# Moving most of a fused kernel's activation loads from SyncE's to GpSimd's DMA queue, and its GELU table load to a later place

## The chip, the core and the metric

One core of one Trainium2 chip. The time is that of one execution on the device in microseconds (us). A time quoted for a kernel is the median of its runs. A trace is taken of one execution by the hardware profiler; its span is some 1.7 us shorter than the run's time. A run over 1.5% above the fastest of its kernel counts as slow.

In the views PE is TensorE (PEld its weight loads), DVE VectorE, ACT ScalarE, POOL GpSimd and SP SyncE. Of TensorE's products, ps_t are transposes, ps_s scores, ps_o outputs of the attention, ps_kv the state from k and v, ps_h and ps_out the two layers of the MLP, and ps_fill products of zeros that keep it busy.

## The reference, cut to what matters

The kernel fuses decaying linear attention with a two-layer MLP. The attention takes q, k, v of shape 4 batches x 8 heads x 768 positions x 64, in float32, block by block of 64 positions; its output is the input of the MLP.

```python
for b in range(nb):                                  # 12 blocks of 64 positions
    intra = einsum(qb, kb) * Dmask                   # within the block
    intra = einsum(intra, vb)
    inter = einsum(qb * lam_pow, kv_state)           # from the blocks before
    out[:, :, sl] = intra + inter
    kv_state = lam_block * kv_state + einsum(kb * rev_pow, vb)
...
h = x @ w_in                                         # 3072 x 512 by 512 x 2048
g = h * sigmoid(1.702 * h)
return g @ w_out                                     # 2048 x 512
```

## The kernel before

The work goes in six "waves" of positions. In waves 0 and 1 (`w < ND`, ND is 2) each half `c` of a wave is the first 256 positions of one batch, from wave 2 on 128 positions of two batches. "Batch 0" and "batch 1" in the texts are the two halves `c` of a wave. The landing buffers kf, qf, vf are float32 tiles of 4096 bytes on each of 128 partitions. The weights go through GpSimd's queue and are converted to bf16 on the way. The k, q and v go through SyncE's, except for one.

```python
def load_one(w, c, nm, src):
    x = ld.tile([P, H, 2 * D], f32, tag=f"{nm}{c}", name=f"{nm}f")
    if w < ND:
        n = H if w or (nm == "v" and c) else H // 2
        for h in range(0, H, n):
            (nc.gpsimd if w == 0 and c and nm == "v" else nc.sync).dma_start(out=x[:, h : h + n], in_=...)
    else:
        nc.sync.dma_start(out=x.rearrange(...), in_=...)
...
    behind = const.tile([1, 2], bf16)        # where the gates write
    behind_q = const.tile([1, 1], f32)
...
def gate_pool(x):                            # GpSimd goes on when x has landed
    nc.gpsimd.tensor_copy(behind_q, x)
def gate_sync(x):                            # SyncE's queue goes on when x has landed
    nc.sync.dma_start(out=behind, in_=x)
...
# for wave 1, batch 0, GpSimd casts v (in two halves); for batch 1 it casts k, and ScalarE v
((pool_copy, pool_copy), (act_copy, act_copy))[c]
...
if w + 2 < NW:                               # wave w+2 is loaded n+20 items into wave w (w = 0)
    side += [(n + (12 if w else 20), (load, w + 2))]
```

## Time and profile before

| | before |
|---|---|
| median of 3 runs | 207.61 us (207.47 to 208.85) |
| span of the profiled run | 206.6 us (its time was 208.35, so it is one of the slower runs) |
| TensorE busy | 96% of the span |
| TensorE's waits at wave 1's start (ps_kv) | none |

The main lines are in the prediction below. Two more rows of the page belong to them: each digit is one fortieth of the span, in tenths of full speed (PEclk, the granted clock of TensorE) or of the busy time of the 16 DMA engines.

### The profile page before, as it was taken

How to read it: one execution, taken by the hardware profiler on the slowest of the kernel's cores; microseconds unless marked ns; L12 is line 12 of the kernel's file. 1: busy time of each engine (PE TensorE's matmuls, PEld its weight loads, DVE VectorE, ACT ScalarE, POOL GpSimd, SP SyncE). 2: the span in 40 equal slices, each digit the busy share in tenths (PEclk: the TensorE clock that was granted, in tenths of full speed). 3: DMA queues.
4: the chain of work that ended last, by engine and by line, in shares of the span. 5: the costliest groups of instructions: out<-in, count | busy, mean ns of one | idle time of the engine just before them, and what ended most of it. 6: DMA issues, size and time to landing. Idle time of an engine off the chain costs nothing.

```text
span 206.6 us, 4263 instructions
## 1 busy us (share of the span) xinstructions
PE 199.1 (96%) x1802; PEld 105.3 (51%) x1825; DVE 89.3 (43%) x160; ACT 86.1 (42%) x158; POOL 17.1 (8%) x38
## 2 busy tenths in 40 slices
PE   7989999999999999999999999999999999999994
PEld 2657544467864464444464444464444454444453
DVE  1784000686952842932743931743841731100121
ACT  4857662157665030565030566021566021565000
POOL 4469000140000000000000000000000000000000
PEclk9999999999999999999999999999999999999999
DMA  5999999999997999979981379961360111100112
GB/s 156 314 232 197 195 206 257 316 274 228 210 226 182 213 261 235 217 169 224 257 234 51 110 180 264 232 184 52 102 151 3 46 59 51 51 0 0 54 51 102
DMA packets 86744, 33.82 MB, mean 164 GB/s; under 512 B 67398, under 2 KB 83654, under 8 KB 86726
## 3 DMA queue, kind: packets, MB, share of 16 engines
q1 hardware_dynamic: 81828, 28.84, 55.2%
q0 software_dynamic: 4896, 4.72, 13.6%
q8 instruction: 14, 0.23, 0.4%
q14 instruction: 4, 0.03, 0.1%
q10 hardware_dynamic: 2, 0.00, 0.0%
HBM read 27.26 MB, written 6.29 MB: 162 GB/s over the span
## 4 chain that ended last, share of the span: by engine, by line
PE 89%; DMA 3%; SPq 3%; DVE 3%; issue 1%; ACT 0%; ACTq 0%
PE ps_out L418 39%; PE ps_h L394 35%; PE ps_h L406 5%; DMA qf<-in_q_dram 3%; SPq L81 3%; PE ps_s L332 2%; PE ps_o L382 2%; PE ps_o L369 1%; DVE o_sb L422 1%; PE ps_t L235 1%; DVE sm L264 1%; PE ps_o L313 1%; PE ps_kv L356 1%; PE ps_s L256 1%; PE ps_o L295 1%
## 5 line engine op out<-in xcount | busy, mean ns | idle before, releaser
L418 PE MATMUL ps_out<-w_out,g_sb 128*128 128x512 bf16 (+2 forms) x400 | 83.8, 362 | 1.1 <-issue 0.6
L394 PE MATMUL ps_h<-xT,w_in 128*128 128x512 bf16 x330 | 73.2, 379 | 0.3
L396 ACT ACTIVATE g_sb<-ps_h 128x512 bf16<-128x512 f32 x84 | 50.1, 597 | 45.2 <-PE ps_h L394 45.2
L418 PEld LDWEIGHTS <-g_sb 128*128 128x128 bf16 x416 | 38.2, 98 | 41.0
L394 PEld LDWEIGHTS <-w_in 128*128 128x128 bf16 x336 | 32.9, 98 | 39.2
L422 DVE COPY o_sb<-ps_out 128x512 f32<-128x512 f32 (+2 forms) x26 | 16.9, 650 | 53.0 <-PE ps_out L418 50.2
L340 DVE SCALAR_TENSOR_TENSOR sm<-ps_s,inv_pow,mask 128x512 bf16<-128x512 f32 x32 | 21.8, 743 | 28.5 <-PE ps_s L332 22.3
L386 ACT CAST xT<-ps_o 128x512 bf16<-128x512 f32 x16 | 8.2, 600 | 37.8 <-PE ps_o L382 37.8
L199 DVE TENSOR_TENSOR ks<-kf,kd_pow 128x256 bf16<-128x256 f32 x8 | 2.9, 420 | 20.6 <-DMA kf<-in_k_dram 17.3
L406 PE MATMUL ps_h<-xT,w_in 128*128 128x256 bf16 x96 | 11.4, 273 | 0.0
L206 DVE TENSOR_TENSOR qs<-qf,q_pow 128x512 bf16<-128x512 f32 x16 | 10.3, 682 | 0.0
L206 DVE TENSOR_TENSOR ks<-kf,k_pow 128x512 bf16<-128x512 f32 x16 | 10.3, 682 | 0.0
L406 PEld LDWEIGHTS <-w_in 128*128 128x128 bf16 x96 | 9.0, 98 | 1.6 <-DVE xT L215 0.2
L264 DVE TENSOR_TENSOR sm<-ps_s,mask_d 128x512 bf16<-128x512 f32 x14 | 8.8, 683 | 0.9 <-PE ps_s L256 0.8
L408 ACT ACTIVATE g_sb<-ps_h 128x512 bf16<-128x512 f32 x12 | 7.2, 598 | 4.3 <-PE ps_h L406 4.3
L144 PE MATMUL ps_fill<-zero 128*128 128x512 bf16 x14 | 6.7, 576 | 1.5 <-DVE zero L114 1.4
L360 DVE SCALAR_TENSOR_TENSOR kv<-kv,blk_pow,ps_kv 128x256 bf16<-128x256 bf16 x12 | 5.0, 476 | 6.0 <-PE ps_kv L356 6.0
L218 ACT COPY kT<-ps_t 128x512 bf16<-128x512 bf16 (+1 forms) x4 | 3.2, 796 | 7.7 <-PE ps_t L235 7.6
L199 DVE TENSOR_TENSOR qs<-qf,qd_pow 128x256 bf16<-128x256 f32 x16 | 5.8, 419 | 1.3 <-DMA qf<-in_q_dram 1.3
L332 PEld LDWEIGHTS <-kT 64*128 64x128 bf16 x128 | 3.6, 94 | 3.4 <-issue 3.4
L215 DVE CAST v_sb<-vf 128x1024 bf16<-128x1024 f32 x8 | 5.1, 683 | 0.0
L332 PE MATMUL ps_s<-qT,kT 64*128 64x128 bf16 x128 | 5.0, 217 | 0.0
(69 smaller groups left out, 93.4 us busy)
## 6 DMA issues: line engine op xcount, KB each, us to landing
kf<-in_k_dram SPq DMA_DIRECT2D x10, 512.0 KB, 5.8
qf<-in_q_dram SPq DMA_DIRECT2D x10, 512.0 KB, 6.5
vf<-in_v_dram SPq DMA_DIRECT2D x10, 512.0 KB, 6.7
out_dram<-o_sb SPq DMA_DIRECT2D x15, 256.0 KB, 2.0
out_dram<-o_sb SPq DMA_DIRECT2D x17, 128.0 KB, 2.4
w_out<-in_moe_w_out_dram POOLq DMA_DIRECT2D x4, 512.0 KB, 12.7
kf<-in_k_dram SPq DMA_DIRECT2D x4, 256.0 KB, 3.1
qf<-in_q_dram SPq DMA_DIRECT2D x4, 256.0 KB, 5.1
```

Of the source, the lines that this page charges most:

```text
L199: eng.tensor_tensor(x.rearrange("p a (r i j d) -> p r j i a d", i=2, j=2, d=D)[:, R, j], f[:, h].rearrange("p i (a d) -> p i a d", a=2), p ...
L206: eng.tensor_tensor(x.rearrange("p b (r i j d) -> p j (b r) i d", i=2, j=2, d=D)[:, j], f.rearrange("p h (a d) -> p (h a) d", a=2).rearran ...
L264: nc.vector.tensor_tensor(sm.rearrange("p i a s -> p i (a s)"), flat, mask_d.rearrange("p o a b s -> p o (a b s)").to_broadcast([P, 2, 2 * ...
L332: nc.tensor.matmul(s2[h][:, b, :], kT[hs, (b % 2) * NP + p, :], qT[hs, (b % 2) * NP + p, :], start=True, stop=True)
L340: nc.vector.scalar_tensor_tensor(sm, s, inv_pow[:, n : n + 1], mask.to_broadcast([P, B, P]), op0=MUL, op1=MUL)
L386: nc.scalar.copy(xT[w][:, p, :], ps_o.rearrange("p b s -> p (b s)"))
L394: nc.tensor.matmul(h, w_in_sb[j][:, kc, i * P : (i + 1) * P], xT[w][:, kc, :], start=(kc == 0), stop=(kc == KC - 1))
L396: nc.scalar.activation(g_of[w][:, fc, :], h, GELU)
L406: nc.tensor.matmul(h[:, u, :], w_in_sb[j][:, kc, i * P : (i + 1) * P], xT[w][:, kc, cols], start=(kc == 0), stop=(kc == KC - 1))
L408: nc.scalar.activation(g_of[w][:, fc : fc + 2, cols], h, GELU)
L418: nc.tensor.matmul(ps_out, g_of[w][:, fc, g * P : (g + 1) * P], w_out_sb[j][:, fc % CW, c0:c1], start=(fc == 0), stop=(fc == FFC - 1))
L422: nc.vector.tensor_copy(o, ps_out)
```

## The change

The intent: give nearly all loads of the first 50 us to one issuer in one order, so that nothing has to be gated, start batch 1's loads of wave 0 earlier, and take the GELU table load out of ScalarE's busiest stretch.

```diff
-                (nc.gpsimd if w == 0 and c and nm == "v" else nc.sync).dma_start(
+                (nc.gpsimd if w or c else nc.sync).dma_start(
...
-            nc.sync.dma_start(out=x.rearrange(...),
+            (nc.gpsimd if w == ND else nc.sync).dma_start(out=x.rearrange(...),
...
-                    if w or c == 0 or nm != "v":
+                    if w or c == 0:
...
-    behind = const.tile([1, 2], bf16)
...
-    def gate_sync(x):
-        nc.sync.dma_start(out=behind, in_=x)
...
-        nc.scalar.activation(warm, q_pow[:, 0, 0:1], GELU)
+        gate_pool(loaded[0, 0, "k"][0:1, H // 2, 0:1])
+        load_one(0, 1, "k", k)
+        load_one(0, 1, "q", q)
+        load_w_in(0)
+        load_one(0, 1, "v", v)
...
-        for nm, copies in (("k", (dve_copy, act_copy)), ("q", (act_copy, dve_copy))):
+        for nm, copies in (("k", (act_copy, act_copy)), ("q", (act_copy, dve_copy))):
...
-                fill(2 - g if nm == "k" else 1 - g)
-        gate_pool(loaded[0, 0, "q"][0:1, H // 2, 0:1])
-        load_w_in(0)
-        load_one(0, 1, "v", v)
+                fill(1 if nm == "k" else 1 - g)
         cast_v(0, 0, (act_copy, act_copy))
+        nc.scalar.activation(warm, q_pow[:, 0, 0:1], GELU)
...
-        fill(3)
+        fill(2)
...
-        gate_sync(w_out_sb[1][0:1, 0, 0:2])
         load(1)
...
-                side += [(n + (12 if w else 20), (load, w + 2))]
+                side += [(n + (12 if w else 8), (load, w + 2))]
```

More of the change, by code (lines that the diff above doesn't have):

```diff
@@ L84, in load_one @@
         else:
-            nc.sync.dma_start(out=x.rearrange("p h (a d) -> p (h a) d", a=2),
+            (nc.gpsimd if w == ND else nc.sync).dma_start(out=x.rearrange("p h (a d) -> p (h a) d", a=2),
                               in_=src[2 * c : 2 * c + 2, :, w * P : (w + 1) * P, :].rearrange("b h s d -> s (b h) d"))
```

## The prediction

> **What bounds the kernel now.** I read the page's engine shares first, then the chain of work that ended last in order of time, and then the start of the kernel engine by engine. The chain's summary:
>
> ```profile
> span 206.6 us, 4263 instructions
> PE 199.1 (96%) x1802; PEld 105.3 (51%) x1825; DVE 89.3 (43%) x160; ACT 86.1 (42%) x158; POOL 17.1 (8%) x38
> PE 89%; DMA 3%; SPq 3%; DVE 3%; issue 1%; ACT 0%; ACTq 0%
> ```
>
> TensorE is 96% busy and 89% of the chain. A transfer is only 3% of it. In order of time (columns: start, duration, what):
>
> ```profile
> 6.21 0.65 SPq L81
> 6.85 0.04 issue
> 6.90 6.48 DMA qf<-in_q_dram
> 13.38 0.02 issue
> 13.40 0.77 DVE qs L199 x2
> 14.17 0.05 issue
> 14.22 0.40 PE ps_t L235 x4
> ...
> 15.24 2.08 DVE sm L264 x4
> 17.32 0.04 issue
> 17.36 0.31 PE ps_o L313 x8
> ...
> 18.57 2.78 PE ps_h L406 x24
> ...
> 203.59 0.29 DVE o_sb L422
> ```
>
> From 18.57 us to 203.59 us the chain is matmuls, one after another, apart from three waits of 0.70 us for an output copy, which the change does not touch. So a change of loads can win only in the first 18.57 us, and there only along q of batch 1: issued last on SyncE, landed at 13.38, cast, transposed, scored, masked, multiplied. Everywhere else it can at best do no harm. GpSimd's timeline shows what the change will load up (start, duration, instruction; in brackets idle time before it and its releaser):
>
> ```profile
> 7.00 0.23 POOL L453 COPY behind_q<-qf 1x1 f32<-1x1 f32 x1 [3.63 <-DMA qf<-in_q_dram]
> 7.17 0.95 POOL L178 DMA_DIRECT2D w_in<-in_moe_w_in_dram  x1
> 8.11 0.92 POOL L81 DMA_DIRECT2D vf<-in_v_dram  x1
> 9.85 2.32 POOL L199 TENSOR_TENSOR ks<-kf,kd_pow 128x256 bf16<-128x256 f32 x4 [0.81 <-ACT v_sb L218]
> 12.12 1.55 POOL L178 DMA_DIRECT2D w_in<-in_moe_w_in_dram  x2
> ...
> 40.39 1.16 POOL L212 CAST v_sb<-vf 128x512 bf16<-128x512 f32 x2 [19.62 <-DMA vf<-in_v_dram]
> ```
>
> One issue keeps GpSimd 0.75 to 0.95 us, also for the 1024 rows of v (0.92). At 40.39 it casts wave 1's v as soon as that lands. Its reader on TensorE (v_sb is an operand) follows closely:
>
> ```profile
> 42.89 0.44 PE L276 MATMUL ps_kv<-v_sb,ks 64*64 64x64 bf16 x16
> ```
>
> **What the Trainium skill says.** (1) "DMA: Bandwidth & Descriptors", Issuing engines are not separate DMA queues: all issuers share the same 16 engines; another issuer saves only sequencer time. Its section Queues, rings and completion order adds that each engine goes round-robin between queues, packet by packet. The first agrees with the trace, the second hardly: between 31 and 34 us, with wave 1's loads issued on SyncE from 30.85 us behind the weights on GpSimd's queue, the DMA view has
>
> ```profile
> q0 software_dynamic: 619, 0.62, 123.5%
> q1 hardware_dynamic: 5, 0.00, 0.3%
> ```
>
> (packets, MB written, share of the engines). So the order is close to the order of issue, whichever the queue. Likewise w_in, issued at 7.17, has no packet before 10 us, while q1 works off its backlog. (2) The same page, Latency and other measured facts, gives about 1 us to the first byte for GpSimd and 0.6 us for SyncE. Here w_in, issued at 12.12 into a nearly empty queue, shows packets from about 14.1: 2 us. (3) "ScalarE: Activation LUTs", What ACT_TABLE_LOAD costs: 1283 ns and a drain of 1380 ns. The trace has 1.28 us for the load and the next instruction right at its end, with no drain seen. (4) "SBUF — State Buffer", SBUF: two separate sides: a vector op in a two-port mode keeps GpSimd from writing descriptors. In the start VectorE runs two-input products and PSUM copies, and the issues there took under 0.95 us, so I add nothing.
>
> **The change part by part.**
>
> Queue of batch 1, wave 0. Removed: four SyncE issues (4.18 to 7.82) and the gate on q. Added: a gate on the second half of k (issued at 1.33, some 3.0 us to landing, so about 4.4) and six GpSimd issues in a row. Estimate: gate copy 0.2, then six issues of 0.75 to 0.95 from about 4.7: GpSimd free at 9.6 to 10.2, against 9.03 before. First packet of k at 4.7 + 2.0 = 6.7, or later; batch 0's 1.57 MB (1.03 MB by 6 us, 0.65 MB from 6 to 8) is through at about 7.7, so nothing starves. The order k, q, w_in, v is the order of issue before, too; the gain is that w_in and v no longer run among the tail of q. By 10 us 2.33 MB had moved; batch 0 plus batch 1's k and q are 2.62 MB; at 0.32 MB/us the rest is through at 10.9. Last data to semaphore was 1.3 us (q's packets nearly gone at 12.1, landed 13.38), so q lands at about 12.2, not 13.38: 1.1 us earlier. VectorE is at its masks until 12.13 before. GpSimd's own casts of k end at 12.2 to 12.6 as before (12.17).
>
> Table behind the v casts. Removed from ScalarE: 1.28 + 0.20 us at 5.80 to 7.29. Added: the same after the v casts. The gap there is 1.52 us (9.85 to 11.37), so it fits: cost nil. Both kT copies go to ScalarE, one 0.42 us copy leaves VectorE; one fill matmul fewer before k's second turn and another later. The q turns start some 0.3 us earlier (7.24 against 7.56), so the four masks of batch 0 start at about 9.2 instead of 9.73 and end at 11.7 instead of 12.2.
>
> The sum in the start. The casts of q end at about 13.0 instead of 14.17, but then the transposes of k and ScalarE's copies (xT, qT, xT) bind: scores at 14.2 instead of 14.77. The masks' last product hangs on ScalarE's second copy, which stands behind batch 1's v cast: v lands at 14.9 to 15.4 (15.4 before). The last product then ends at 16.8 to 17.1 instead of 17.3. Start: 0.2 to 0.7 us won, middle 0.45.
>
> Waves 1 and 2. Removed: SyncE's gate on w_out and twelve issues. Added: twelve issues on GpSimd, in order, before its casts of wave 1. A GpSimd transfer waits for the eighth one before it, as the order of instructions with waits shows. So the last v of wave 2 waits for k of wave 1, batch 1, and only behind it comes the cast of wave 1's v. Estimate: the weights end at 33.4 as before; 0.524 MB at 0.34 MB/us is 1.55 us each, plus 1.3: k 36.2, q 37.8, v 39.3, then k of batch 1 at 40.8. One issue of 2048 rows, by 0.75 to 0.92 us for 512 and 1024 rows, some 1.0 to 1.3 us: GpSimd free at about 42.0, two casts of 0.58 until 43.2. Before they ended at 41.55. TensorE wants them at 42.89, less 0.45 for its earlier start: 42.4. So it waits about 0.8 us, between 0 and 1.5. The later casts of k (2.33 us, until 45.5) meet a turn at 45.76 and should just hold. Wave 2's data come earlier than before, where VectorE needs it from 53.41 on: no gain.
>
> Sum: 207.61 - 0.45 + 0.8 is 208.0 at the centre of the estimates; with a faster stream of the larger packets of GpSimd's queue (v moved at about 0.35 MB/us, w_in is read faster) k lands at 40.2 and the wait is 0.2, which gives 207.4. I take 207.5.
>
> **The rivals.** A: the start gains all of q's 1.1 us and the waits of wave 1 stay hidden: 206.4. For it: q is the chain's transfer, and the fill and load positions look tuned. Against it: two other engines bind within 0.6 us of q. B: GpSimd is held up, by descriptors of 2048 rows at 2 us or more each or by a full descriptor ring: with 2 us each it is free at about 45, the v cast ends at 46.2, TensorE waits 3.7 us: 211. For it: no run shows such an issue. Against it: v's 1024 rows cost no more than w_in's 512 (0.92 and 0.95). C: nothing shows, since TensorE is full from 18.57 us and the same bytes come in the same order: 207.6.
>
> **Range and chances.** B's worst is past 2% (211.8), A's best is far from it the other way (203.5): 18 us of start cannot give 4. Faster by over 2%: 0.02. Slower by over 2%: 0.05. Within: 0.93. Time 207.5, range 206.0 to 209.2.
>
> **What would show each step.** Right: q of batch 1 cast by 13.2 us, the first dense matmuls of ps_h at about 18.1; the table load inside ScalarE's gap with the kv copy no later than 11.5; a wait of TensorE at ps_kv near 42.5 us that ends with GpSimd's v cast, if it shows at all. Wrong: GpSimd's issues longer than 1.5 us; v of batch 0 landing after 8.7 us because k of batch 1 takes its place in the engines; a dry stretch of the DMA engines near 7 us; GpSimd free later than 43 us.

## More of the kernel before

The pools are laid out in the order of the code: all `const` tiles, with the two gate tiles near their end, and behind them the landing buffers of the pool `ld`. In the built program a gate tile takes 32 bytes of each partition.

```profile
PEclk9999999999999999999999999999999999999999
DMA  5999999999997999979981379961360111100112
```

TensorE has its full clock throughout. The DMA engines are busy for 90% or more from 5 to 62 us, and for 70% or more until some 108 us. So for that time every byte waits its turn, and what counts is the order of the transfers and the rate at which they go.

SyncE's timeline shows how the kernel before lives with that (start, duration, instruction):

```profile
40.36 5.25 SPq L85 DMA_DIRECT2D kf<-in_k_dram  x2
45.70 3.93 SPq L85 DMA_DIRECT2D qf<-in_q_dram  x2
49.72 5.45 SPq L85 DMA_DIRECT2D vf<-in_v_dram  x2
```

Wave 2's six loads keep SyncE's sequencer for 14.8 us, from 40.36 to 55.17, as it seems because the queue takes them only as fast as the engines work them off. That costs nothing here: TensorE has no wait for wave 2, and GpSimd casts wave 1 meanwhile.

## The result and the profile after

The changed kernel takes 213.62 us (median of 4 runs, 213.41 to 214.45) against 207.61. The ratio is 1.0283, with a 95% interval of 1.0235 to 1.0331: slower by more than 2%. A ratio here is always the mean time of one kernel's fast runs over that of the other's of the same rounds on the same chip, so it is not quite the ratio of the medians.

The page after, with the rows that answer to those of before (span, clock, chain):

```profile
span 211.7 us, 4295 instructions
PEclk9999999987999999999999999999999999999999
PE 76%; DMA 17%; POOL 4%; issue 1%; POOLq 0%; SPq 0%; DVE 0%
```

Transfers are now 17% of the chain instead of 3%, and GpSimd is 4% of it; GpSimd is busy 15% of the span instead of 8%. There is a dent in the clock at slices 9 and 10, some 42 to 53 us. The waits of TensorE (total, times, longest) name the place:

```profile
PE ps_kv L275 <- POOL v_sb L211: 3.2, 2, 2.9
```

GpSimd's timeline shows why its cast comes late:

```profile
36.93 1.16 POOL L85 DMA_DIRECT2D kf<-in_k_dram  x1 [1.86 <-DMA w_out<-in_moe_w_out_dram]
38.84 1.15 POOL L85 DMA_DIRECT2D qf<-in_q_dram  x1 [0.75 <-DMA kf<-in_k_dram]
...
42.62 1.15 POOL L85 DMA_DIRECT2D vf<-in_v_dram  x1 [0.82 <-DMA vf<-in_v_dram]
44.30 1.15 POOL L85 DMA_DIRECT2D vf<-in_v_dram  x1 [0.53 <-DMA kf<-in_k_dram]
45.44 1.17 POOL L211 CAST v_sb<-vf 128x512 bf16<-128x512 f32 x2
```

The issues of wave 2 take 1.15 us each. Before the last four, GpSimd waits for one of wave 1's transfers (before the first two, for weights). Wave 1's v has landed at 41.93, yet its cast begins at 45.44, because two issues stand before it. In the kernel before it began at 40.39. The windows view shows what follows (stretch, length, busy us and count of PE, PEld, DVE, ACT, POOL, granted clock, DMA share, GB/s):

```profile
44.00:46.00 2.00, 0.00 (x0) 0.00 (x0) 0.00 (x0) 0.00 (x0) 1.70 (x3) 1.00 1.06 277
47.00:49.00 2.00, 2.00 (x47) 1.36 (x43) 1.29 (x3) 1.24 (x5) 1.89 (x4) 0.50 1.09 227
50.00:52.00 2.00, 2.00 (x17) 1.05 (x15) 1.54 (x5) 0.57 (x1) 0.00 (x0) 1.00 1.05 223
```

TensorE is idle for about 2.9 us, and then has half its clock until 50 us. At half clock for some 3 us it does about 1.5 us of work less. Waiting (3.2) and clock (1.5) make most of the 5.1 us by which the span grew. (By the medians it is 6.0 us; the profiled run before was a slower one.)

The Trainium skill has this in "TensorE: Matmul & The Clock Gate", section HAM oscillation: its rule is that TensorE should have no idle gaps over some 3.4 us, beyond which the clock gate throttles it. The trace agrees in kind, with an idle stretch somewhat shorter (2.9 us by the wait view). In the run waves_only below a longest single wait of 1.6 us was followed by half the clock as well.

Between 34 and 42 us, when waves 1 and 2 stream in, GpSimd's queue moved (packets, MB, share of the 16 engines)

```profile
q0 software_dynamic: 759, 2.39, 105.9%
```

That is 2.39 MB in 8 us or 299 GB/s, with the engines full. Wave 1's transfers of 512 KB landed at 38.31, 40.12, 41.93 and 43.77, 1.8 us apart. The prediction had reckoned with 340 GB/s and 1.55 us.

In the start the changes worked as foreseen in the one trace: the first dense ps_h at 18.08 us instead of 18.50, and the table load in ScalarE's gap:

```profile
10.18 1.28 ACT L474 ACT_TABLE_LOAD   x1
11.48 0.20 ACT L474 ACTIVATE warm<-q_pow 128x1 f32<-128x1 f32 x1
11.59 0.35 ACT L285 CAST kv<-ps_kv 128x256 bf16<-128x256 f32 x1
```

### The profile page after: what moved, and what is told of

Read it like the earlier page. It is cut to its first block, busy times and chain, and to the rows that moved or that the text cites. A ratio compares the mean times of both kernels' runs of the same rounds, so it can differ in the third digit from the quotient of the medians.

```text
span 211.7 us, 4295 instructions
## 1 busy us (share of the span) xinstructions
PE 202.5 (96%) x1823; PEld 105.4 (50%) x1823; DVE 89.4 (42%) x159; ACT 86.7 (41%) x159; POOL 32.7 (15%) x54
## 4 chain that ended last, share of the span: by engine, by line
PE 76%; DMA 17%; POOL 4%; issue 1%; POOLq 0%; SPq 0%; DVE 0%
PE ps_out L417 35%; PE ps_h L393 29%; DMA vf<-in_v_dram 12%; DMA w_in<-in_moe_w_in_dram 4%; PE ps_h L405 3%; PE ps_s L331 2%; PE ps_o L381 2%; DMA kf<-in_k_dram 2%; POOL vf L85 1%; PE ps_o L368 1%; POOL kf L81 1%; PE ps_s L255 1%; PE ps_kv L355 1%; POOL qf L81 1%; POOL v_sb L211 1%
## 5 line engine op out<-in xcount | busy, mean ns | idle before, releaser
L417 PE MATMUL ps_out<-w_out,g_sb 128*128 128x512 bf16 (+2 forms) x416 | 87.0, 365 | 0.0
L385 ACT CAST xT<-ps_o 128x512 bf16<-128x512 f32 x16 | 8.2, 600 | 37.8 <-PE ps_o L381 37.8
L405 PE MATMUL ps_h<-xT,w_in 128*128 128x256 bf16 x96 | 11.5, 273 | 0.0
L217 ACT COPY kT<-ps_t 128x512 bf16<-128x512 bf16 (+1 forms) x5 | 3.8, 756 | 10.7 <-PE ps_t L234 10.7
L144 PE MATMUL ps_fill<-zero 128*128 128x512 bf16 x13 | 6.2, 572 | 1.4 <-DVE zero L114 1.4
L275 PE MATMUL ps_kv<-v_sb,ks 64*64 64x64 bf16 x128 | 3.8, 198 | 3.3 <-POOL v_sb L211 3.2
L275 PEld LDWEIGHTS <-ks 64*64 64x64 bf16 x128 | 3.2, 113 | 4.6 <-issue 4.4
```

What stands on the lines that cost most here:

```text
L385: nc.scalar.copy(xT[w][:, p, :], ps_o.rearrange("p b s -> p (b s)"))
L405: nc.tensor.matmul(h[:, u, :], w_in_sb[j][:, kc, i * P : (i + 1) * P], xT[w][:, kc, cols], start=(kc == 0), stop=(kc == KC - 1))
L417: nc.tensor.matmul(ps_out, g_of[w][:, fc, g * P : (g + 1) * P], w_out_sb[j][:, fc % CW, c0:c1], start=(fc == 0), stop=(fc == FFC - 1))
```

## The experiments

The first theory: GpSimd issues in order, and its issues of wave 2 stand before its casts of wave 1. The first rivals: the start part of the change; the mere place of the casts; the clock. A further rival came up only when the parts did not add up. All runs gave correct results. The medians, with the kernel before beside each ("start 256" is the start of kf in its partition, past a multiple of 256 bytes, in the built program):

| run | what differs | us | before | ratio (95%) | start 256 |
|---|---|---|---|---|---|
| start_only | only the start of the change | 208.24 | 207.61 | 1.0013 (0.9984 to 1.0043) | 0 |
| waves_only | only waves 1 and 2 | 210.20 | 207.61 | 1.0117 (1.0067 to 1.0166) | 0 |
| casts_first | changed, wave 2 issued behind all casts | 212.49 | 207.61 | 1.0221 (1.0185 to 1.0257) | 224 |
| fill_wait | changed, fill matmuls in the wait | 213.58 | 207.61 | 1.0284 (1.0241 to 1.0327) | 224 |
| v2_last | changed, wave 2's v behind the casts | 210.66 | 208.18 | 1.0103 (1.0051 to 1.0156) | 224 |
| w2_sync | changed, wave 2 on SyncE | 209.32 | 208.18 | 1.0053 (0.9984 to 1.0123) | 0 |
| v_dve | changed, wave 1's v cast on VectorE | 212.32 | 208.18 | 1.0202 (1.0136 to 1.0267) | 224 |
| n20 | changed, wave 2 between v and k casts | 217.22 | 208.18 | one run | 224 |
| w1_sync | changed, wave 1 on SyncE | 218.99 | 207.81 | 1.0526 (1.0470 to 1.0582) | 0 |
| table_only | before, with the table moved | 208.37 | 207.81 | 1.0002 (0.9959 to 1.0044) | 0 |
| v_first | start_only, v ahead of w_in | 208.40 | 207.81 | 1.0008 (0.9972 to 1.0045) | 0 |
| waves_table | waves_only and the table moved | 210.13 | 207.65 | 1.0099 (1.0057 to 1.0141) | 0 |
| after_aligned | changed, 32 bytes put back | 210.15 | 207.80 | 1.0116 (1.0084 to 1.0148) | 0 |
| before_shift | before, landing buffers moved | 210.94 | 207.80 | 1.0142 (1.0100 to 1.0185) | 224 |
| v2_aligned | v2_last, 32 bytes put back | 208.74 | 207.80 | 1.0022 (0.9974 to 1.0070) | 0 |
| w_align | before, weights' tiles on 256 too | 207.82 | 207.80 | 1.0011 (0.9974 to 1.0048) | 0 |
| at_64 | changed, buffers at 64 | 214.35 | 207.68 | 1.0332 (1.0293 to 1.0370) | 64 |
| at_128 | changed, buffers at 128 | 213.94 | 207.68 | 1.0305 (1.0259 to 1.0351) | 128 |

Slow, and so left out of the ratios, are one run each of start_only (211.10), casts_first (215.71) and v2_aligned (212.09), and one of the kernel before (211.59).

### The two halves of the change alone

start_only keeps the start and puts waves 1 and 2 back on SyncE with its gate. waves_only does the reverse.

```diff
# start_only, against the changed kernel
-(nc.gpsimd if w or c else nc.sync)
+(nc.gpsimd if w == 0 and c else nc.sync)
-(nc.gpsimd if w == ND else nc.sync)
+nc.sync
+    behind = const.tile([1, 2], bf16)
+        gate_sync(w_out_sb[1][0:1, 0, 0:2])
         load(1)
-(12 if w else 8)
+(12 if w else 20)
# waves_only, against the kernel before; the tile `behind` stays
-(nc.gpsimd if w == 0 and c and nm == "v" else nc.sync)
+(nc.gpsimd if w or (c and nm == "v") else nc.sync)
-nc.sync                                # wave 2
+(nc.gpsimd if w == ND else nc.sync)
-        gate_sync(w_out_sb[1][0:1, 0, 0:2])
-(12 if w else 20)
+(12 if w else 8)
```

> Only the first 18 us of the change: batch 1 of wave 0 on GpSimd's queue, the gate on k, the later table load, the fewer fills. Waves 1 and 2 are loaded on SyncE behind the gate on w_out as before. Theory (the loss lies wholly in GpSimd's late cast of wave 1's v and the clock drop that follows): the first dense ps_h run starts at about 18.1 us instead of 18.5, the ps_kv products near 42.5 to 43 without a wait, clock 1.00 throughout, and 207.0 to 207.4 us against 207.6. Rival (the new start itself costs, for instance through the queue it leaves behind): 209 us or more.

> Only the other half: the start as before, waves 1 and 2 on GpSimd's queue without the gate, wave 2 issued ahead of GpSimd's casts. Theory: the whole loss is here; ps_kv of wave 1 waits until about 46.5 us, the clock falls to half for some 3 us after it, and the time is 213.2 to 214.2 us, since what the start wins is taken up by the wait. Rival (start and waves each cost a part): clearly under 212 us.

The start alone costs nothing and gains nothing that the times show: 1.0013, and 208.24 us where 207.0 to 207.4 were expected. In its trace the first dense ps_h comes at 17.98, half a microsecond earlier, but has waited 0.4 us for w_in.

The second w_in is issued at 11.77, landed at 17.94, and now binds. The trace of waves_only, whose start is that of the kernel before, has its first dense ps_h at 18.03. So the 0.42 us between my one trace before and my one trace after lie within what one kernel does from run to run.

The waves alone cost 1.2%, not the 2.8% expected. GpSimd's v cast stands at 43.39 there, 2 us earlier than in the changed kernel, and TensorE waits 1.9 us. Of its four runs two have a mean clock of 0.999 (209.08 and 209.27 us) and two of 0.991 to 0.992 (211.59 and 211.13). The loss of clock so goes with about 2 us. But a mean clock of 0.992 stands also in single runs of kernels whose trace shows no such wait: one of six of start_only, one of six of w_align, and two of the 54 of the kernel before (209.55 and 211.59). With the long wait the loss is regular (all four runs of the changed kernel), but the wait is not its only cause. The halves did not add up.

### Moving the casts and the issues against each other

```diff
# casts_first                    # n20                        # v2_last
-(12 if w else 8)                -(12 if w else 8)             -(12 if w else 8), load all
+(12 if w else 26.7)             +(12 if w else 20)            +(n + 8, (load, 2, "kq")), (n + 26.7, (load, 2, "v"))
# v_dve
-((pool_copy, pool_copy), (act_copy, act_copy))[c]             # and the v cast 7 items later
+((dve_copy, dve_copy), (act_copy, act_copy))[c]
```

> The changed kernel with one move: wave 2's six issues stand behind GpSimd's casts of wave 1 (v and k) in its order; every load stays on GpSimd's queue. Theory (in-order GpSimd, held by the wait of each issue for the eighth transfer before it): the v cast starts when v lands, about 42 us, and ends at 43.2; ps_kv waits about 0.2 to 0.7 us; no clock drop; 207.5 to 208.5 us. Rival (the slower landing of wave 1 on this queue is the cause, 38.3, 40.1, 41.9, 43.8 us): the wait stays over 2 us and the time over 210.

> The changed kernel with wave 2's loads at their old place in the program, between GpSimd's casts of v and of k. Theory: the v cast starts at 42, wave 2's six issues follow until about 50, the casts of k end after 52, and TensorE waits 5 us or more at the turn of k: 212 to 215 us, DMA engines not quite full between 43 and 48. Rival (the place of the loads does not matter): 213.6 with the wait still at ps_kv.

> The changed kernel, with only the two v loads of wave 2 moved behind GpSimd's casts of wave 1; k and q of wave 2 stay ahead of them. Theory now (GpSimd has to do two things at about 42 us: hand out wave 2's loads so that the full DMA engines don't run dry, and cast wave 1; in one in-order queue one of them comes late, and the last two issues are what the v cast loses): GpSimd's v cast starts at about 42 us, the DMA engines keep four transfers of backlog and stay full from 45 to 50 us, no wait of TensorE over 0.8 us at ps_kv nor at wave 2's ps_s, 207.3 to 208.8 us. Rival (any load of wave 2 on this queue costs, by the larger packets or the slower stream): over 210 us.

> The changed kernel with wave 1's first v cast taken from GpSimd to VectorE (two copies, just ahead of the products that read it); every load as in the change. Theory: the wait at ps_kv shrinks to under 1 us, since v lands at about 42, but the next job in GpSimd's order, the casts of k for batch 1, is still held behind wave 2's issues and ends at about 47.8, where TensorE wants it at about 46: a wait of 1.5 to 2.5 us at ps_t takes its place, and the time is 208.8 to 210.3 us. Rival (only the v cast matters): 207.5 to 208.3.

casts_first takes the wait at ps_kv away, and yet is 2.2% slower than the kernel before. GpSimd's timeline and TensorE's new wait:

```profile
41.82 1.17 POOL L211 CAST v_sb<-vf 128x512 bf16<-128x512 f32 x2 [10.09 <-DMA vf<-in_v_dram]
...
45.92 2.35 POOL L85 DMA_DIRECT2D kf<-in_k_dram  x2
```

```profile
PE ps_s L331 <- DMA qT<-qs: 3.0, 3, 1.6
```

The cast now follows v's landing at once. But wave 2 is issued from 45.92 to 52.8, up to 8 us later, and the DMA engines fell to 44% busy between 45 and 50 us, where the changed kernel has them full. That time is missing later: wave 2's transposes come late, and TensorE waits 3.0 us at ps_s, from 67.7 us on. The wait has moved and not gone. My expectation of 207.5 to 208.5 was wrong. (A part of what is left in this run and in the next three has the further cause that is shown below.)

In n20 the six issues stand between GpSimd's v casts and its k casts. The k casts come at 50.12 instead of 46.57, and TensorE waits 6.1 us for them (one run of unknown state, but the wait itself, of which one piece is 5.0 us, is plain; 212 to 215 us were expected).

v_dve gives the v cast to VectorE. TensorE's waits fall to 0.8 us at ps_kv and 1.4 us at the turn of k, but it gains only 0.6% on the changed kernel, 2 us less than expected. A gap of 1.6 us without any visible cause stands in TensorE at 54.4 us. v2_last lets GpSimd issue k and q of wave 2, cast, and then issue v. Nothing waits at ps_kv for GpSimd, the engines stay full, and 3 of the 6 us are gone, though 207.3 to 208.8 us were expected. Again a gap of 1.1 us stands at 53.8 us. I could not explain these gaps then; what the traces show of them stands under what stays open.

### The clock

```diff
# fill_wait: in the wait at ps_kv TensorE multiplies zeros
             if c == 0:
+                fill(14, "a")
                 d_one(w, c)
```

> The changed kernel with 14 fill matmuls (3.0 us) ahead of wave 1's first ps_kv, so that TensorE is not idle while it waits. It tells the idle time from the clock. Theory (3.5 us of waiting, then 3.1 us at half clock, worth 1.5 us): ps_kv still starts near 46.7 us, the granted clock stays 1.00, and the time is 211.8 to 212.4 us. Rival (the clock follows something else, or the whole 5 us is waiting): the clock still falls or the time stays within 0.4 us of 213.6.

The 14 matmuls ran at 43.15 to 46.34, and the clock stayed at 1.00 throughout. The turn of wave 1's k came 1.2 us earlier than in the changed kernel. But TensorE then stood 1.1 us at 55.06 without a visible cause, and the time is that of the changed kernel: 213.58, not the expected 211.8 to 212.4. Three of its four runs have a mean clock of 1.00 and one 0.984, where all four of the changed kernel have 0.984 to 0.992. So filling the wait prevents the fall of the clock; that this fall costs the whole kernel its 1.5 us is not shown by this run.

### Giving wave 2 to another issuer

```diff
# w2_sync, against the changed kernel
-(nc.gpsimd if w == ND else nc.sync)        # wave 2
+nc.sync
+nc.sync.dma_start(out=behind_w, in_=loaded[1, 0, "k"][0:1, 0, 0:2])   # its gate
-(12 if w else 8)
+(12 if w else 20)
```

> The changed kernel with wave 2's loads given back to SyncE, held there until wave 1's k of batch 0 has landed (a 4-byte-wide gate transfer); wave 1 stays on GpSimd. Theory: GpSimd is free from about 32 us, casts v when it lands (about 42), wave 2 is issued between 38 and 53 us, no wait of TensorE over 0.8 us: 207.3 to 208.8 us. Rival (wave 1 itself, on GpSimd's queue, lands too late): ps_kv waits over 1.5 us and the time is over 209.5.

GpSimd waits for v's landing alone and casts at 40.52, after 8.1 us of waiting for it. There is no wait at ps_kv, and 1.0053 cannot be told from the kernel before (207.3 to 208.8 us were expected, 209.32 came). What was left in this trace is 1.6 us for w_in in the start. At the time I took this run for a clean proof that wave 2's place on GpSimd is the whole loss. It was not clean. The gate's tile, that I had put in for wave 2, moved the buffers as well, as turned out below.

> The changed kernel, but wave 1 goes back to SyncE's queue, behind its gate on w_out; wave 2 stays on GpSimd's, where it was. If it is the order on GpSimd that costs (each of its issues waits for the eighth of its own transfers before it), then the eighth before wave 2's loads are now weights, batch 1's v and the like, landed by about 36 us, and no longer wave 1's k and v: GpSimd is through with its six issues by about 41 us, casts wave 1's first v as soon as that lands (39 to 40.5 us), TensorE does not wait at ps_kv and its clock stays at 1.0. Time within 1% of the kernel before: 206.8 to 209.0. If instead it is enough that wave 2 is issued early and on GpSimd (issue cost, crowding of wave 1's loads by wave 2's), wave 1's k and v land late as in the changed kernel or later (v at 41.9 us or after), TensorE still waits 2 us or more, and the time is 211 or more.

w1_sync put wave 1 on SyncE behind its gate and left wave 2 on GpSimd. I had overlooked that nothing held wave 2 back now: GpSimd issued it from 19.60 us on, and wave 1 only went out from 31.08. TensorE waited 8.3 us at the turn of wave 1's k, its v landed at 49.28, and 218.99 us is the worst time of all. The expectation failed through its design. GpSimd's issues were then waiting for weights and not for wave 1. But the order of issue is only a part of it. Between 35 and 40 us, when both queues have work, they moved (packets, MB, share)

```profile
q0 software_dynamic: 416, 1.50, 89.5%
q1 hardware_dynamic: 368, 0.19, 14.2%
```

The two queues send nearly packet for packet (163 and 166 between 38 and 40 us), but a packet of GpSimd's queue carries 4096 bytes and one of SyncE's 512 in this trace. So wave 1 got about an eighth of the bytes of wave 2.

### What of the start does it? And a start that might gain

```diff
# table_only, against the kernel before: only the second part of the change's start
-        nc.scalar.activation(warm, q_pow[:, 0, 0:1], GELU)
-... (("k", (dve_copy, act_copy)), ...        +... (("k", (act_copy, act_copy)), ...
+        nc.scalar.activation(warm, q_pow[:, 0, 0:1], GELU)      # behind batch 0's v casts
# waves_table: waves_only with the same
# v_first, against start_only
+        load_one(0, 1, "v", v)
         load_w_in(0)
-        load_one(0, 1, "v", v)
-        mlp1_half(0, 0, 0)                  # and again behind batch 1's ps_kv
```

> The kernel before with only the second part of the change's start: the GELU table loaded behind batch 0's v casts, both kT copies of k on ScalarE, the fill matmuls as in the changed kernel; all loads as before. If the table load fits ScalarE's gap, as the prediction has it, nothing is lost: q of batch 1 still lands at about 13.4 us and binds, so nothing is won either, 207.0 to 208.2 us, the first dense ps_h at 18.4 to 18.7 us. If the load pushes the kv copy or the v casts, ps_h comes at 19 us or later and the time is 0.5 us or more above the kernel before.

> The changed start with waves 1 and 2 as before, and two repairs: batch 1's v is issued ahead of the first w_in, and batch 1's ps_kv and its keep are put ahead of the first half of mlp1 on TensorE, so that w_in may land later. With waves 1 and 2 as before the start's gain of 0.4 us in the first dense product should be kept and the wait of 0.4 us for w_in, which ate it in the run with the changed start only, should go: 206.9 to 207.5 us against 207.6, ratio 0.996 to 0.999, too little to be told apart from the same unless the interval is narrow. If w_in still lands after its product is wanted, the wait stays or grows, and the time is that of the kernel before or up to 1 us above it.

> The whole change but for its first part: waves 1 and 2 go through GpSimd as in the changed kernel, the table load stands behind batch 0's v casts, but k and q of batch 1 of wave 0 stay on SyncE, with the gate on q as before. The run with the waves alone lost 1.2%, the whole change 2.8%, and the start alone nothing, so the parts do not add up; this tells which part of the start makes up the rest. If it is the loads of batch 1 on GpSimd (its later issues stand about 0.9 us later, so the weights and wave 1 land later, and TensorE's wait passes the length at which its clock drops), this kernel is like the one with the waves alone: v casts on GpSimd at 43 to 44 us, ps_kv waits 1.5 to 2.5 us, 209.0 to 211.6 us, ratio about 1.012. If it is the table load and the copies (TensorE wants wave 1 sooner, so waits longer and loses its clock), ps_kv waits 2.5 us or more and the time is 212.5 to 214.

The table load may stand where it likes: 1.0002. In table_only VectorE cast batch 1's q at 11.70 without waiting, though it still went through SyncE. So not even the landing at 13.38 that the prediction starts from is a constant of the kernel. v_first removes the wait for w_in and puts one of 0.9 us for v in its place; it gains nothing (206.9 to 207.5 us were expected). waves_table behaves as waves_only does (1.0099), so neither the table nor the copies make up the missing 1.6%. By this reckoning it had to be batch 1's k and q on GpSimd.

### The 32 bytes

It was something else. I sorted all traces by the rate between 34 and 42 us. The traces with wave 1 on GpSimd's queue fall into two groups. In the changed kernel, casts_first, fill_wait, v2_last, v_dve and n20 the rate is near 300 GB/s. In waves_only, waves_table and w2_sync it is near 380. The engines are full in both. In the built programs the groups differ in the last column of the table above. (No trace shows an address; the tile sizes in the code give the same steps.) With `gate_sync` the change removes its tile `behind`, 32 bytes, and every buffer behind it in SBUF slides down, those of the transposes and of the output too: kf starts at byte 64,736 of its partition instead of 64,768, which is 253 x 256.

```diff
# after_aligned, against the changed kernel; v2_aligned: v2_last with the same line
+    pad = const.tile([1, 2], bf16)
     behind_q = const.tile([1, 1], f32)
# before_shift, against the kernel before
+    pad = const.tile([1, 112], bf16)       # 224 bytes
# at_64 and at_128, against the changed kernel
+    pad = const.tile([1, 48], bf16)        # and [1, 80]
# w_align, against the kernel before: the weights' tiles on 256 as well
+    pad_w = const.tile([1, 48], bf16)      # ahead of w_in_sb
+    pad = const.tile([1, 80], bf16)        # ahead of behind_q
```

> The changed kernel with a dead tile of 4 bytes where the tile of SyncE's gate was, so that all landing buffers start on a multiple of 256 bytes again, as in the kernel before; no instruction differs. If the 32 bytes are the reason, wave 1's transfers land about 1.4 us apart (queue at 370 to 385 GB/s between 34 and 42 us, against 300), GpSimd casts wave 1's v at 43 to 44 us, ps_kv waits about 2 us, and the time is that of the run with the waves alone: 209.0 to 211.0 us, ratio 1.007 to 1.016. If the loads of batch 1 on GpSimd's queue are the reason, nothing changes: 300 GB/s, 213 to 214.5 us, ratio 1.025 to 1.032.

> The kernel before with a dead tile of 224 bytes ahead of the landing buffers, so that these start at 224 past a multiple of 256 bytes, as in the changed kernel; no instruction differs. If the alignment of the buffers sets the rate of the loads, SyncE's loads of wave 1 move slower than 335 GB/s between 34 and 42 us (290 to 310 if they suffer as GpSimd's do), and as the kernel has some 2 us to spare at wave 1, the time is 207.6 to 210, most of it from later waves. If SyncE's rows of smaller pieces do not suffer, or alignment is not the reason, the rate stays at 305 to 340 and the time at 207.3 to 208.5.

> The run in which wave 2's two v loads stand behind GpSimd's casts (210.66 us), with the 32 bytes put back as well. If the alignment explains the rest of its loss, the queue moves 370 us-MB-scale rates, that is 0.37 to 0.385 MB/us between 34 and 42 us, GpSimd casts wave 1's v at 41 us or before, and the time is 207.3 to 209.0. If the gap of 1.1 us in TensorE at about 54 us is of another making it shows again and the time is 209.0 to 210.3.

> The kernel before with two dead tiles, so that the weights' tiles too start on a multiple of 256 bytes (they start at 160 past one in both kernels), landing buffers still on one; no instruction differs. If alignment sets the rate of the weights' loads as well, the stretch from 20 to 30 us moves more than 205 GB/s, w_in lands earlier, wave 1 begins up to 2 us earlier; as TensorE is full from 18.5 us on, the time gains at most the half microsecond that w_in can cost at the start: 207.0 to 207.6, ratio 0.996 to 1.0. If the weights' loads are bound by what they read and convert, nothing changes: 1.000 within 0.003.

> The changed kernel with a dead tile of 96 bytes ahead of the landing buffers, which then start at 64 past a multiple of 256 bytes. If a multiple of 64 bytes is enough, the queue moves 370 to 385 GB/s between 34 and 42 us and the time is that of the aligned one, 209.0 to 211.3 us, ratio 1.007 to 1.016. If it takes one of 256, or of 128, the rate is about 300 GB/s and the time 212.7 to 214.5, ratio 1.023 to 1.032.

> The changed kernel with a dead tile of 160 bytes ahead of the landing buffers, which then start at 128 past a multiple of 256 bytes. If a multiple of 64 or of 128 is enough, 370 to 385 GB/s between 34 and 42 us and 209.0 to 211.3 us; if it takes one of 256, about 300 GB/s and 212.7 to 214.5 us.

These kernels differ in addresses alone from the ones that they are made of. The new tiles are never touched. The queue that loads wave 1, between 34 and 42 us, in after_aligned:

```profile
q0 software_dynamic: 869, 3.01, 102.9%
```

in the kernel before:

```profile
q1 hardware_dynamic: 4925, 2.49, 104.3%
```

and in before_shift:

```profile
q1 hardware_dynamic: 3828, 1.93, 90.1%
```

On a multiple of 256 bytes GpSimd's queue moves 3.01 MB in 8 us, 376 GB/s. At 224, 64 or 128 past one it moves 2.39, 2.37 and 2.41 MB, 296 to 301 GB/s. So a multiple of 64 or of 128 bytes is not enough. SyncE's queue with its smaller packets suffers too, but less than its 1.93 against 2.49 MB suggest: it held the engines for 90.1% there, and in the other kernels that load an aligned wave 1 through SyncE alone it moved 2.22 to 2.56 MB. For each full share of the engines it moved 2.14 MB, against 2.32 to 2.39 in those, 8 to 10% less.

The 32 bytes are worth about 1.7% to the changed kernel (1.0283 against 1.0116, intervals apart), its longer wait and its regular loss of clock included. The shift by 224 bytes costs the kernel before 1.4%; which of the moved buffers costs it is not separated. (Expected were 290 to 310 GB/s and 207.6 to 210 us; 241 and 210.94 came.) at_64 and at_128 repeat the changed kernel's loss. Where the kernel before loses its 1.4% is only partly seen: wave 1's v cast is at 42.73 instead of 40.39, and TensorE waits 1.1 us for a transpose at ps_s, which it did not before, and 1.5 us in all for casts of k (0.3 us before).

The Trainium skill bears on it in "DMA: Bandwidth & Descriptors", section How a descriptor splits into AXI transactions: a descriptor is split into transactions of 256 bytes, and one that does not start on a multiple of 256 begins with a transaction from the boundary below, so that it can need one more. That agrees in the size of the step, 256. The page words this for reads; here the side off 256 is the one that is written. By its count, as an estimate, a descriptor of 4096 bytes would need 17 transactions in place of 16, or 6% more. If instead each contiguous run of the source is one, 512 bytes in wave 1 and 256 in wave 2, it would be 3 in place of 2, and 2 in place of 1. Measured, the aligned rate is a quarter higher (376 / 299 is 1.26). In the packed traces the median packet of 4096 bytes on GpSimd's queue took 174 ns aligned and 229 ns not between 36 and 42 us, and 195 against 306 to 314 ns in wave 2 (45 to 55 us). So the shorter runs lose more, as the second count has it, but less than it says. The page gives the condition, and these runs the size; the mechanism behind the size is open.

With the buffers aligned, what is left of the change's loss is GpSimd's order. In after_aligned:

```profile
36.96 1.16 POOL L85 DMA_DIRECT2D kf<-in_k_dram  x1 [1.71 <-DMA w_out<-in_moe_w_out_dram]
38.11 2.29 POOL L85 DMA_DIRECT2D qf<-in_q_dram  x2
40.77 2.39 POOL L85 DMA_DIRECT2D vf<-in_v_dram  x2 [0.38 <-issue]
43.16 1.17 POOL L212 CAST v_sb<-vf 128x512 bf16<-128x512 f32 x2
```

Now the transfers of wave 1 come in faster than GpSimd can issue, and the wait for the eighth before it is nearly gone. It is the issues themselves that fill the time from 36.96 to 43.16: five of 1.15 us and 0.4. TensorE waits 1.0 us at ps_kv and 1.3 us for w_in in the start. v2_aligned takes the two v issues from before the casts: the cast begins at 40.12, no single wait over 0.5 us is left but that of the fill matmuls at the start, no gap shows at 54 us, and 1.0022 cannot be told from the kernel before (one of its four runs was slow and is left out). Its interval (up to 1.0070) and after_aligned's (from 1.0084) do not overlap, so by the fast runs the place of those two issues costs about 0.9%. If the run left out (212.09 us, clock 0.982) were counted, the means would differ by half of that; but the runs with a mean clock of 0.997 or more agree with it, 207.61 and 207.75 against 209.38 to 210.23.

w_align shows that the weights' loads are not helped by the same care: 205 GB/s between 26 and 30 us with it as without, and the same time. No kernel here beats the one before.

## Why the prediction was wrong, point by point

**The stream rate.** The step "k 36.2, q 37.8, v 39.3, then k of batch 1 at 40.8", from 0.34 MB/us, failed. The landings were 38.31, 40.12, 41.93 and 43.77. The rate was 0.30 MB/us, because the buffers had lost their alignment. The prediction's hope for "a faster stream of the larger packets of GpSimd's queue" was right for aligned buffers (0.376) and came out as its opposite. I read the removal of `behind` in the diff as the removal of a gate, and did not ask what stood behind it in memory. This is worth 1.7 of the 2.8%.

**The end of the weights.** "The weights end at 33.4 as before" was too early for the issue of the next load: GpSimd waited for the last w_out until 36.9 with aligned buffers and without. (33.4 was also misread: in the kernel before, GpSimd's queue still has 61 packets between 34 and 35 us, and landing is later.)

**GpSimd's last issue.** The sum "GpSimd free at about 42.0" was short by 3.4 us; it was 45.44. The issue itself was well estimated (1.15 us against 1.0 to 1.3). The landing before it was 3.0 us late, and 0.5 us more passed between the landing and the issue. With aligned buffers GpSimd is free at 43.16, and there the limit is not the eighth transfer before, as the prediction had it, but the row of issues. The mechanism was right in the main: in-order issues before the cast, and TensorE waiting at ps_kv for GpSimd's v cast near 42.5 us. Its size was off: 3.2 us against 0.8.

**The clock.** Left out. A wait of 2.9 us brought half the clock for 3 us.

**The start.** The working came nearly true in its single trace (q's casts from 11.68, dense ps_h at 18.08, kv copy at 11.59 against "no later than 11.5"). One of its signs of being wrong came too: ScalarE waited 0.64 us for batch 0's v and cast it at 9.03 instead of 8.71, so that it landed after 8.7. The gain of 0.45 us is not confirmed: start_only 1.0013, table_only 1.0002, v_first 1.0008. The step that fails is "binds": w_in lands just when the shorter start wants it, which the list of what binds next did not have.

**Two readings of the queues.** "So the order is close to the order of issue, whichever the queue" fits the lines shown there; w1_sync, with 416 packets against 368, shows that it is no rule. The "2 us" to w_in's first packet was misread: its packets, the first of 768 bytes, begin at 13.69, 1.6 us after the issue at 12.12, and v was still in the queue.

**Rival B** came nearest: it named GpSimd held until 45 us and 211 us. Its reasons, issues of 2 us or a full ring, did not come. The chance of 5% was too small, because all the slack in wave 1 (about 1.3 us from GpSimd's cast to its reader) had been spent by my own central estimate. The step "Wave 2's data come earlier than before ... no gain" held; but casts_first showed that wave 2 cannot simply be issued late either.

The sum as the runs have it, in ratios: 1.4% for the alignment (before_shift), 1.2% for the waves in GpSimd's order (after_aligned), 0 for the start, together 2.6 of 2.8% (the 1.4% is of another kernel; on the changed kernel the alignment is worth 1.7%).

What stays open: the gaps of 1.1 to 1.6 us in TensorE near 54 us, in fill_wait, v2_last and v_dve only. The packed traces show a likely cause that I had overlooked. In all three TensorE stops behind 1208 recorded instructions of its own, although 28 more of these stand ahead of it in fill_wait, so that it is other work that stops there. And in each, a packet of 16,384 bytes on a queue of the kind "instruction" ends 1.4 to 1.7 us before TensorE goes on (at 54.79 in fill_wait, 53.23 in v2_last, 54.48 in v_dve). In v2_aligned it ends at 48.59, 3.1 us before TensorE comes to that place, and there is no gap. So its instructions probably came late behind the loads, which would also explain why fill_wait and v_dve gained so little; no run tests this. Open too are why a start off a multiple of 256 costs a quarter, and what the half clock costs in the end.

## What to carry to other kernels

Removing a tile moves everything that is allocated behind it: compare the start addresses of the DMA buffers in the two built programs, and keep them on a multiple of 256 bytes. Before putting loads on an engine that also computes, write down its order of issues and computations, with the duration of every issue, and look for the first computation that now stands behind an issue. Where two queues have work at once, compare the sizes of their packets. And when the parts of a change do not add up, look for what differs between the runs that belongs to none of the parts.

## What the Trainium skill lacked or had wrong

- "DMA: Bandwidth & Descriptors", How a descriptor splits into AXI transactions: has the boundary of 256 bytes, but not what it costs a load into SBUF. Measured: 376 GB/s on a multiple of 256, 296 to 301 at 64, 128 and 224 past one (rows of 4096 bytes, engines full). Its transaction count would give 6% for a descriptor of 4096 bytes and half more for one of 512 (estimates).
- "SBUF — State Buffer", Operand start alignment: says that it is about legality and timed nothing. A line on speed belongs there: a shift by 32 bytes cost the changed kernel 1.7%, one by 224 bytes the kernel before 1.4%.
- "DMA: Bandwidth & Descriptors", Queues, rings and completion order: the round-robin by packets showed in w1_sync (416 against 368 packets in 5 us), not in the kernel before between 31 and 34 us (619 against 5). What the section lacks is that the bytes then follow the size of the packets: 1.50 against 0.19 MB.
- The same page, Latency and other measured facts: about 1 us to the first byte for GpSimd. The second w_in's first packet came 1.5 to 1.7 us after the start of its issue (kernel before, changed kernel, start_only, waves_only, table_only, v_first).
- "ScalarE: Activation LUTs", What ACT_TABLE_LOAD costs: 1.28 us agrees; no drain was seen (warm at 11.48, right behind 10.18 + 1.28).
- "TensorE: Matmul & The Clock Gate", HAM oscillation: half the clock came after an idle stretch of 2.9 us by the wait view, and after a shorter one in waves_only, below the 3.4 us of the page; in two of waves_only's four runs only.
- No page has the cost of an issue of 512 KB on GpSimd (1.15 us for wave 2's, 0.88 to 0.96 for wave 1's).
